# A third fold of the odd rows of a Fourier transform in seven of eight sequences: four row tiles, products of 94 or 95 columns

## The chip, the cores and the metric

The kernel runs on one core of one Trainium2 chip. The metric is the device time of one execution in microseconds (us); shown are medians of several runs. The engines are TensorE (PE; its weight loads are listed apart as PEld), VectorE (DVE), ScalarE (ACT), GpSimd (POOL) and SyncE (SP, which issues most DMAs). Each takes its own instructions in the order in which the program gave them, and they meet at semaphores.

## The reference

```python
x: (8, 3008, 256) float32          # batch, sequence, width
X = np.fft.fft(x, axis=1)
X = np.fft.fft(X, axis=2)
attn = X.real                      # (8, 3008, 256)
h = attn.reshape(24064, 256) @ w_in      # w_in (256, 2048)
r = np.maximum(h, 0.0)
out = (r * r) @ w_out                    # w_out (2048, 256)
```

So: the real part of a two-dimensional Fourier transform of every sequence, and then a two-layer network with a squared Relu.

## The kernel before, in words

**Two jobs interleaved.** The kernel goes through 8 sequences (b), each of 6 blocks of 251 (or 250) frequencies k, each block in 8 iterations j: 384 iterations in all. An iteration is `front` (two halves h; each makes two matmuls into a PSUM tile `ph`, of which there are two buffers; DVE adds them up in three instructions, `he` and twice `g`), `combine` (ACT: Relu and Square over `g`; POOL: four sums `s`) and, two iterations later, `back` (seven matmuls that add up in `mA` to `mD`). At the end of a block, `gather` and `store` bring the result out. The width transform is folded into the first weight matrix (`G1`, `G2`), so that the sequence transform alone is left to be made for each sequence: `Pt` (cosine part) and `Qt` (sine part).

**The transform of sequence b+1 is made while sequence b runs.** `ahead(b)` writes out a list of pieces, each with a weight that stands for its time. `between()`, called after each half h of a front, takes pieces from the list at an even pace, so that the list is used up at the sequence's end. For one iteration in each block (two iterations after the block's start) no pieces are taken. The first sequence has fewer calls for its list (53 against 78), because its first 8 iterations also convert the weights, and takes pieces at a quarter of the pace until iteration 16. Its list is longer too: it has the column of the middle frequency (`fold_columns`, `dft_ops(None)`) and the tables' reordering (`part_table`).

**The sequence transform by folds.** Only rows n from 0 to S/4 are needed, since x[n], x[S-n], x[S/2-n] and x[S/2+n] come as four rows of one tile and are added and subtracted first (`fold`: `f_s`, `f_d`, `f_sc`, `f_dc`, `f_w`; about 4 us of DVE for a tile). The rows stand in classes: n divisible by four, n = 2 mod 4, other small odd ones, and a last class (c = 3, `ODD0` and after) which holds the rows from S/8 + 1 to S/4, 376 of them. For each of cosine and sine (`which`) and for even and odd k (`kp`) a `group` makes an `even_n` product, joins it (`join_4`, `join_2`), makes the `odd_n` product, and joins both (`join_1`). That is four groups for each sequence. The products go into PSUM tiles `pd` (two buffers).

**The second fold.** In sequences 1 to 7 the class c = 3 is folded once more, row r with row 2*HALF - r, by `f_turn`, `f_even`, `f_sine` and `f_odd` in `fold`: the rows that come mirrored are loaded in blocks of 32 in reverse order, and `stream_shuffle` reverses each block. The even columns are added and subtracted, the odd ones turned through an angle that the table `turn` holds for every row. The products then have half of the columns (189 or 188), in two parts. `once_more` makes them: for c = 3, two parts by two row tiles of 128 rows, four matmuls in each group. Class c = 2 is treated so too, with rows tiles `TWO` and `TWO + 1` of 94 rows, and products of 94 or 95 columns. For kp = 1, each such product needs a copy to SBUF by ACT and two DVE instructions (`join_odd`) to put it together; for kp = 0 the two parts are written into every other column of PSUM directly.

**What sets the order.** The program order on each engine is the order in which the pieces are emitted. A piece that waits holds up whatever its engine was given after it. The x tiles are loaded by SP three tiles ahead (`NX`), each load emitted with `f_d` of an earlier tile. `make_turn` fills `turn` by ACT at iteration 8 (i == NJ), before that iteration's front.

Of the kernel before, what the change touches and what calls it, by code (L numbers as in the profile page):

```python
# [8 lines left out]
F32 = mybir.dt.float32  # L9
# [5 lines left out]
R = 32  # L15
# [67 lines left out]
def kernel(  # L83
# [54 lines left out]
    ODD0 = NT - 3  # L138
    HALF = S // 16
    REST = HALF - P  # L140
    ODD = [[(0, 0, P)],
           [(p, 2 * HALF - p - R, R) for p in range(0, P, R)],
           [(0, P, H // 2)] + [(H // 2 + p, 2 * HALF - P - p - R, R) for p in range(0, H // 2, R)]]
    assert H == P and REST <= H // 2 and TILES[ODD0][0] == 3 and TILES[ODD0 + 1][1] == TILES[ODD0][1] + P

    TWO = ODD0 - 2
    HALF2 = S // 32
    ROWS2 = TILES[TWO][3]
    assert TILES[TWO][0] == TILES[TWO + 1][0] == 2 and HALF2 <= ROWS2 < HALF2 + R and ROWS2 % R == 0

    def load_x(b, t):
        c, r0, step, rows = TILES[t]
        if b and c == 3:
            xt[b, t] = xp.tile([P, 4, D], F32, name="xt", tag="x")
            for p, first, count in ODD[t - ODD0]:
                nc.sync.dma_start(out=xt[b, t][p:p + count], in_=x[b, S // 8 + 1 + first:S // 8 + 1 + first + count])
            return
        if b and t == TWO + 1:
            xt[b, t] = xp.tile([P, 4, D], F32, name="xt", tag="x")
            for p in range(0, ROWS2, R):  # L160
                at = TILES[TWO][1] + step * (2 * HALF2 - p - R)
                nc.sync.dma_start(out=xt[b, t][p:p + R], in_=x[b, at:at + step * (R - 1) + 1:step])
            return

        while rows % 15 and rows % 16 and r0 + step * rows < NROW:
            rows += 1

        pool, tag = (gp, "g") if b == 0 and t < NT - NX else (xp, "x")
        xt[b, t] = pool.tile([P, 4, D], F32, name="xt", tag=tag)
        nc.sync.dma_start(out=xt[b, t][0:rows], in_=x[b, r0:r0 + step * (rows - 1) + 1:step])  # L170

    cosd = const.tile([P, 2, P], F32, name="cosd")
# [152 lines left out]

    turn = const.tile([P, 3, 3], F32, name="turn")

    def make_turn():
        for i, t in enumerate((ODD0, ODD0 + 1, TWO)):
            for a, tab in enumerate((cosT, sinT, sinT)):  # L330
                r = slice(0, TILES[t][3])
                nc.scalar.mul(turn[r, a, i:i + 1], tab[r, 1, PLACE[t]:PLACE[t] + 1], -1.0 if a == 2 else 1.0)

    rows_used = const.tile([P, 1], F32, name="rows_used")
    nc.vector.memset(rows_used, 0.0)
    nc.vector.memset(rows_used[0:REST], 1.0)

    def part_table(tab, t):


        nk, at = NC[0][TILES[t][0]], PLACE[t]
        rows = TILES[t][3]
        v = tab[0:rows, 0, at:at + nk]
        a = op.tile([P, nk], F32, name="tp", tag="os")[0:rows]
        nc.scalar.mul(a, v, rows_used if t == ODD0 + 1 else 1.0)
        nc.scalar.copy(v[:, 0:(nk + 1) // 2], a[:, 0::2])
        nc.scalar.copy(v[:, (nk + 1) // 2:], a[:, 1::2])

    def columns(tab, t, part):

        nk, at = NC[0][TILES[t][0]], PLACE[t]
        nq = (nk + 1) // 2
        return tab[:, 0, at + part * nq:at + (nk if part else nq)]

    NE = B - 1
# [20 lines left out]
    def fold(b, t):  # L376


        odd, two = b > 0 and t >= ODD0, b > 0 and t == TWO + 1
        r = slice(0, P if odd else ROWS2 if two else TILES[t][3])  # L380
        st = {}
# [12 lines left out]
        def f_d():  # L394
            v = xt[b, t]
            tt(out=new(fp, "fd", [P, 2, D])[r], in0=v[r, 0::3], in1=v[r, 1:3], op=ALU.subtract)
            if b > 0 and b * NT + t + NX < B * NT:
                load_x(*divmod(b * NT + t + NX, NT))

# [29 lines left out]
        ops = [(0.9, f_s), (0.9, f_d), (0.7, f_sc), (0.6, f_dc), (1.1, f_w)]  # L429
        if not (odd or two) or t == ODD0:  # L430
            return ops, None


        i = 2 if two else t - ODD0 - 1
        rows = slice(0, (P, REST, HALF2)[i])

        def f_turn():
            w = w_of(t)
            if i != 1:
                st["v"], st["w"] = w_of(t - 1), w  # L440
                nc.vector.stream_shuffle(w[r], w[r], REVERSE)
            else:
                st["v"], st["w"] = w, w_of(NT)
                nc.vector.stream_shuffle(st["w"][0:H // 2], w[H // 2:P], REVERSE)
                nc.gpsimd.memset(st["w"][H // 2:P], 0.0)
            spare("f0", "f0")
            nc.scalar.copy(st["f0"][rows], st["v"][rows, 0])

        def spare(nm, tag):
            st[nm] = fp.tile([P, D], F32, name=nm, tag=tag, bufs=1)  # L450
            return st[nm]

        def sine(to, src, signs):
            for part, a in zip(PART, signs):
                nc.scalar.mul(to[rows, part], src[rows, 1, part], turn[rows, 1 + a, i:i + 1])

        def f_even():
            v, w, a = st["v"][rows, 0], st["w"][rows, 0], st["f0"][rows]
            tt(out=v, in0=a, in1=w, op=ALU.add)
            tt(out=w, in0=a, in1=w, op=ALU.subtract)  # L460

        def f_sine():
            sine(spare("f1", "f1"), st["w"], (0, 1))
            sine(spare("f2", "f0"), st["v"], (1, 0))

        def f_odd():
            for nm, u in (("f1", "v"), ("f2", "w")):
                u = st[u][rows, 1]
                nc.vector.scalar_tensor_tensor(out=u, in0=u, scalar=turn[rows, 0, i:i + 1], in1=st[nm][rows],
                                               op0=ALU.mult, op1=ALU.add)  # L470

        return ops + [(0.8, f_turn), (1.3 if odd else 0.7, f_even), (0.2, f_sine)], (1.4 if odd else 1.2, f_odd)

    def dft_ops(b):
# [7 lines left out]
        def group(kp, which):  # L482
# [25 lines left out]
            def even_n():  # L508
                st["ps"] = psd.tile([P, 512], F32, name="pd", tag="d")[0:n]
                for c, at, nk in EVEN:  # L510
                    if b and c == 2:
                        st["half"] = once_more(st["ps"][:, at:], c, nk)
                    else:
                        product(st["ps"][:, at:at + nk], c)
                copy_4()
# [49 lines left out]

            def once_more(ps, c, nk):

                nq = (nk + 2) // 2 if kp else (nk + 1) // 2
                pairs, rows = ((((TWO, TWO + 1),), HALF2), (((ODD0, ODD0 + 1), (ODD0 + 2, NT)), P))[c == 3]
                for part in range(2):  # L570
# [3 lines left out]
                    else:  # L574
                        tab, o = (cosT, sinT)[which], part
                        to = ps[:, part:nk:2]
                    for i, pair in enumerate(pairs):
                        nc.tensor.matmul(to, folded[b, pair[part != which]][0:rows, kp, PART[which]][:, 0:n],  # L578
                                         columns(tab, pairs[0][i] if c == 3 else TWO, o)[0:rows],
                                         start=i == 0, stop=i == len(pairs) - 1)  # L580
                if not kp:
# [3 lines left out]
                return a, ps[:, nq:2 * nq]  # L585

            def odd_n():
                ps = psd.tile([P, 512], F32, name="pd", tag="d")[0:n]
                st["odd"] = ps[:, 0:n0]
                if b is None:  # L590
                    return product(ps[:, 0:n0], 3)
                st["odd"] = once_more(ps, 3, n0)

# [31 lines left out]
            if b and kp:  # L625
                ops.insert(4, (0.5, lambda: join_odd("odd", n0)))
                ops.insert(2, (0.4, lambda: join_odd("half", n1)))
            return ops

# [161 lines left out]
    def ahead(b):  # L791
        start, *groups = dft_ops(b)
        if b == 1:

            tables = [(0.3, lambda tab=tab, t=t: part_table(tab, t)) for t in (TWO, ODD0, ODD0 + 1)
                      for tab in (cosT, sinT)]
            groups = [(1.5, fold_columns)] + dft_ops(None) + tables + groups
        groups.insert(0, start)

        pieces = []  # L800
        for ops, last in [fold(b, t) for t in range(NT)] + [(groups + [(0.0, lambda: load_e(b))], None)]:
            if held:
                ops.insert(3, held.pop())
            if last:
                held.append(last)
            pieces += ops
        return pieces

    held = []

# [130 lines left out]
    for i in range(len(steps) + LAG + 4):  # L941
        if i < len(steps):
            b, k0, n, j = steps[i]
            if i == NJ:
                for t in range(NX):
                    load_x(1, t)
            if NJ <= i < NJ + NT:
# [92 lines left out]
```

## Time and profile before

| | |
|---|---|
| median of 3 runs | 1938.28 us (1938.12 to 1938.69) |
| span of the profiled execution | 1936.6 us |
| granted TensorE clock, mean | 1.000 |
| PE busy, 242 to 1694 us (windows of 48 to 242 us) | the whole of each window |
| fronts and backs of an iteration on PE | 22 records of 251 columns, 4.67 us |
| period of a sequence (710.24 to 943.21 us, the same product twice) | 232.97 us |
| DMA, mean share of the engines in the middle of the run | 0.11 |

The profile is one execution. An instruction's row tells its source line, engine, operation, the tiles it writes and reads, its shape, the count, the busy time, the mean length and the idle time of the engine before it. PE's rows overlap, since a matmul's end is modelled; its pace is read from the differences of starts. An fp32 matmul stands in the trace as two records. The weight loads (PEld) run beside the matmuls.

### The profile page before, as it was taken

To read this page: it belongs to the slowest core of one execution; us is meant where nothing else is said; L and a number is where in the kernel's file an instruction comes from. 1 tells how busy PE (TensorE), PEld (TensorE's weight loads), DVE (VectorE), ACT (ScalarE), POOL (GpSimd) and SP (SyncE) were. 2 spreads that over 40 slices of the span, in tenths; PEclk is the share of its full clock that TensorE was granted. 3 is DMA by queue.
4 is the path that set the end of the run, shared out by engine and by line. 5 is a ranking of instruction groups with operands and counts; after the bars stand their busy time and mean duration, and the time that the engine had idled before them with its cause. 6 is when DMAs were issued, how large, how long until landed. Compare 5 with 4: busy or idle time off the path is not lost.

```text
span 1936.6 us, 27913 instructions
## 1 busy us (share of the span) xinstructions
PE 1922.7 (99%) x9266; PEld 1708.9 (88%) x9266; DVE 1424.4 (74%) x3502; ACT 939.5 (49%) x1134; POOL 1185.6 (61%) x1708
## 2 busy tenths in 40 slices
PE   8999999999999999999999999999999999999999
PEld 7788888888988899888998889888898888988887
DVE  8998867777677776787667776777767787655554
ACT  2855554544445544445444454445544454444443
POOL 0047646676567665766667665667756776556655
PEclk9999999999999999999999999999999999999999
DMA  8341101111011101111011100111001100000000
GB/s 216 115 48 41 39 8 51 33 32 27 27 41 31 38 12 30 39 41 28 11 35 47 36 20 11 42 48 28 20 17 52 33 11 22 28 12 11 22 11 22
DMA packets 145783, 69.56 MB, mean 36 GB/s; under 512 B 129309, under 2 KB 136423, under 8 KB 145638
## 3 DMA queue, kind: packets, MB, share of 16 engines
q1 hardware_dynamic: 145186, 66.87, 13.3%
q8 instruction: 73, 1.20, 0.3%
q0 software_dynamic: 176, 0.65, 0.1%
q14 instruction: 72, 0.59, 0.1%
q10 hardware_dynamic: 276, 0.26, 0.0%
HBM read 43.03 MB, written 24.69 MB: 35 GB/s over the span
## 4 chain that ended last, share of the span: by engine, by line
PE 95%; DVE 3%; DMA 1%; issue 0%; SPq 0%; ACT 0%; DVEq 0%
PE ph L664 17%; PE ph L665 16%; PE mC L717 16%; PE mA L717 16%; PE mB L717 16%; PE mD L717 8%; PE pd L578 2%; PE pd L501 1%; DMA cosT<-in_cos_s_dram 0%; DVE m L274 0%; DVE he L667 0%; DMA cosd<-in_cos_d_dram 0%; DVE fd L272 0%; DVE g L670 0%; PE mA L704 0%
## 5 line engine op out<-in xcount | busy, mean ns | idle before, releaser
L679 ACT ACTIVATE g<-g 128x1004 f32<-128x1004 f32 (+1 forms) x384 | 399.4, 1040 | 783.6 <-DVE g L670 419.1
L667 DVE SCALAR_TENSOR_TENSOR he<-Et,gE,ph 128x251 f32<-128x251 f32 (+1 forms) x768 | 361.6, 471 | 385.4 <-PE ph L665 382.0
L687 POOL TENSOR_TENSOR s<-g 128x251 f32<-128x251 f32 (+1 forms) x376 | 249.0, 662 | 640.6 <-ACT g L680 507.2
L664 PE MATMUL ph<-Pt,G 128*128 128x251 f32 (+1 forms) x1536 | 451.9, 375 | 0.2 <-DVE g L670 0.2
L665 PE MATMUL ph<-Qt,G 127*128 127x251 f32 (+1 forms) x1536 | 451.3, 374 | 0.0
L680 ACT ACTIVATE g<-g 128x1004 f32<-128x1004 f32 (+1 forms) x384 | 399.3, 1040 | 12.1
L717 PE MATMUL mC<-s,wsum 128*128 128x251 f32 (+1 forms) x1504 | 381.4, 374 | 0.0
L717 PE MATMUL mA<-g,wout 128*128 128x251 f32 (+1 forms) x1504 | 379.9, 374 | 0.0
L669 DVE TENSOR_TENSOR g<-he,ph 128x251 f32<-128x251 f32 (+1 forms) x768 | 320.5, 417 | 54.5 <-DVE he L667 0.9
L665 PEld LDWEIGHTS ph<-Qt,G 127*128 127x128 f32 x1536 | 291.3, 190 | 35.7
L664 PEld LDWEIGHTS ph<-Pt,G 128*128 128x128 f32 x1536 | 286.7, 189 | 36.2 <-DVE dc L547 1.3
L717 PEld LDWEIGHTS mC<-s,wsum 128*128 128x128 f32 x1504 | 285.5, 190 | 34.5
L670 DVE TENSOR_TENSOR g<-he,ph 128x251 f32<-128x251 f32 (+1 forms) x768 | 314.1, 409 | 0.0
L717 PEld LDWEIGHTS mA<-g,wout 128*128 128x128 f32 x1504 | 282.6, 189 | 35.0 <-issue 0.3
L689 POOL TENSOR_TENSOR s<-g 128x251 f32<-128x251 f32 (+1 forms) x376 | 303.3, 807 | 0.0
L688 POOL TENSOR_TENSOR s<-s,g 128x251 f32<-128x251 f32 (+1 forms) x376 | 280.1, 745 | 29.5
L690 POOL TENSOR_TENSOR s<-g,s 128x251 f32<-128x251 f32 (+1 forms) x376 | 260.6, 693 | 0.0
L717 PE MATMUL mB<-g,wsum 128*128 128x251 f32 (+1 forms) x752 | 220.4, 374 | 0.0
L717 PE MATMUL mD<-s,wout 128*128 128x251 f32 (+1 forms) x752 | 220.3, 374 | 0.0
L717 PE MATMUL mB<-s,wout 128*128 128x251 f32 (+1 forms) x752 | 219.9, 374 | 0.0
L717 PEld LDWEIGHTS mB<-g,wsum 128*128 128x128 f32 x752 | 142.5, 190 | 17.5
L717 PEld LDWEIGHTS mD<-s,wout 128*128 128x128 f32 x752 | 141.9, 189 | 17.7
(139 smaller groups left out, 1353.9 us busy)
## 6 DMA issues: line engine op xcount, KB each, us to landing
out_dram<-os SPq DMA_DIRECT2D x376, 56.0 KB
xt<-in_x_dram SPq DMA_DIRECT2D x25, 384.0 KB
xt<-in_x_dram SPq DMA_DIRECT2D x63, 128.0 KB
Et<-e_dram SPq DMA_DIRECT2D x7, 752.5 KB
xt<-in_x_dram SPq DMA_DIRECT2D x9, 512.0 KB
out_dram<-os SPq DMA_DIRECT2D x288, 6.8 KB
raw<-in_moe_w_in_dram SPq DMA_DIRECT2D x16, 256.0 KB
raw<-in_moe_w_out_dram SPq DMA_DIRECT2D x16, 256.0 KB
```

The source lines that it names most:

```text
L664: nc.tensor.matmul(hP, G1[:, fs], pt[:, ks], start=True, stop=True)
L665: nc.tensor.matmul(hQ, G2[0:P - 1, fs], qt[0:P - 1, ks], start=True, stop=True)
L667: nc.vector.scalar_tensor_tensor(out=t, in0=et[:, ks], scalar=gE[:, fc:fc + 1], in1=hP, op0=ALU.mult, op1=ALU.add)
L669: tt(out=g[:, h, 0, 0:n], in0=t, in1=hQ, op=ALU.add)
L670: tt(out=g[:, h, 1, 0:n][:, ::-1], in0=t, in1=hQ, op=ALU.subtract)
L679: act(v, v, AF.Relu)
L680: act(v, v, AF.Square)
L687: gt(out=s1, in0=g21, in1=g22, op=ALU.add)
L688: gt(out=s2, in0=s1, in1=g11, op=ALU.subtract)
L689: gt(out=s3, in0=g11, in1=g21, op=ALU.subtract)
L690: gt(out=s4, in0=g12, in1=s2, op=ALU.subtract)
L717: nc.tensor.matmul(acc[nm][:, i, 0:n], w, v[:, 0:n], start=j == 0 and i == 0, stop=j == NJ - 1, skip_group_check=True)
```

## The change

In sequences 1 to 7 the class c = 3 is folded a third time, row n with S/8 - n. There are now four row tiles of 96 rows (94 used), named av, aw, bv and bw, instead of three of 128, 128 and 120; each passes through `fold`. Then `once` (what `f_turn` to `f_odd` did) joins av with aw and bv with bw, and, as before, the two tiles of class 2; and `twice` joins the two pairs: sums and differences of halves of the even-k columns (`even`), a turn of the differences by a second angle (`sine` on ACT, `turned` on DVE), and sums and differences of the odd-k columns (`copies` on ACT, `odd_v` and `odd_w`). `twice_more` makes the products: four matmuls in each group still, but each of 94 or 95 columns with 94 rows. For kp = 0 they are written to every fourth column of PSUM, and `join_turned` (one ACT copy, two DVE instructions) puts two of the four parts together.

The table `turn` gets a fourth angle, computed by three DVE instructions from two that ACT wrote, and scaled by ACT. The tiles are taken in another order (`ORDER`), and `ahead` weaves the steps of `once` and `twice` between the steps of later folds. The weights of the list for one sequence are the times written beside the pieces.

```diff
+    NL = ODD0 + 4
+    ODD = [[(0, 0, ROWS2)],
+           [(p, 4 * HALF2 - p - R, R) for p in range(0, ROWS2, R)],
+           [(p, 2 * HALF2 - p - R, R) for p in range(0, ROWS2, R)],
+           [(0, 2 * HALF2, ROWS2)]]
...
+    ORDER = [TWO, TWO + 1, 0, *range(ODD0, NL), 1]
...
     def make_turn():
-        for i, t in enumerate((ODD0, ODD0 + 1, TWO)):
+        for i, t, kp, k in ((BY_AC, ODD0, 1, 0), (BY_TWO, TWO, 1, 0), (BY_AB, ODD0, 0, 1)):
             for a, tab in enumerate((cosT, sinT, sinT)):
-                r = slice(0, TILES[t][3])
-                nc.scalar.mul(turn[r, a, i:i + 1], tab[r, 1, PLACE[t]:PLACE[t] + 1], -1.0 if a == 2 else 1.0)
+                r = slice(0, ROWS2)
+                nc.scalar.mul(turn[r, a, i:i + 1], tab[r, kp, PLACE[t] + k:PLACE[t] + k + 1], -1.0 if a == 2 else 1.0)
+        c, z = (turn[0:ROWS2, a, BY_AC:BY_AC + 1] for a in range(2))
+        for a, (u, v, op) in enumerate(((c, z, ALU.add), (c, z, ALU.subtract), (z, c, ALU.subtract))):
+            to = turn[0:ROWS2, a, BY_BD:BY_BD + 1]
+            tt(out=to, in0=u, in1=v, op=op)
+            nc.scalar.mul(to, to, 0.5 ** 0.5)
...
+    def twice(v, w, v2, w2):
...
+        def begin():
+            a = st["a"] = spare("f0")
+            nc.scalar.copy(a[:, p], v[:, 0, p])
+            nc.scalar.copy(a[:, q], w[:, 0, q])
+
+        def even():
+            butterfly(v[:, 0, p], v2[:, 0, p], st["a"][:, p])
+            butterfly(w[:, 0, q], w2[:, 0, q], st["a"][:, q])
+
+        def sine():
+            f, f2 = st["f"] = spare("f1"), spare("f0")
+            for to, u, part, a in ((f, w2, p, SIN), (f2, w, p, LESS), (f, v2, q, LESS), (f2, v, q, SIN)):
+                nc.scalar.mul(to[:, part], u[:, 0, part], by(BY_AB, a))
+
+        def turned():
+            f, f2 = st["f"]
+            for u, part, to in ((w, p, f), (w2, p, f2), (v, q, f), (v2, q, f2)):
+                mix(out=u[:, 0, part], in0=u[:, 0, part], scalar=by(BY_AB, COS), in1=to[:, part],
+                    op0=ALU.mult, op1=ALU.add)
+
+        def copies():
+            st["a"], st["b"] = spare("f0"), spare("f1")
+            nc.scalar.copy(st["a"], v[:, 1])
+            nc.scalar.copy(st["b"], w[:, 1])
+
+        def odd_v():
+            butterfly(v[:, 1], v2[:, 1], st["a"])
+
+        def odd_w():
+            butterfly(w[:, 1], w2[:, 1], st["b"])
...
+            def twice_more(ps):
...
+                av, aw, bv, bw = (folded[b, ODD0 + i] for i in range(4))
+                if kp:
+                    nq = (n0 + 2) // 2
+                    spots = [(tab, part, ps[:, i * nq + part:(i + 1) * nq:2])
+                             for i, tab in enumerate((cosT, sinT)) for part in range(2)]
+                    ws = (aw, bw, bv, av) if which else (av, bv, bw, aw)
+                else:
+                    tab = (cosT, sinT)[which]
+                    spots = [(tab, 0, ps[:, 0:n0:4]), (tab, 1, ps[:, 2:n0:4]),
+                             (cosT, 0, ps[:, 1:n0 + 1:4]), (sinT, 0, ps[:, 3:n0:4])]
+                    ws = (bw, aw, bv, av) if which else (av, bv, aw, bw)
+                for (tab, part, to), w in zip(spots, ws):
+                    cols = quarters(tab, part)
+                    nc.tensor.matmul(to, w[0:HALF2, kp, PART[which]][:, 0:n], cols[:, cols.shape[-1] - to.shape[-1]:],
+                                     start=True, stop=True)
...
+            def join_turned():
+                a, up, down = st["turned"]
+                tt(out=up, in0=a, in1=down, op=ALU.add)
+                if which == 1:
+                    tt(out=down, in0=down, in1=a, op=ALU.subtract)
+                else:
+                    tt(out=down, in0=a, in1=down, op=ALU.subtract)
...
+        two = later(lambda: once(w(TWO), w(TWO + 1), BY_TWO))((0.1, 0.9, 0.2, 1.0))
+        first = later(lambda: once(w(av), w(aw), BY_AC))((0.1, 0.9, 0.2, 1.0))
+        second = later(lambda: once(w(bv), w(bw), BY_BD) + twice(w(av), w(aw), w(bv), w(bw)))(
+            (0.1, 0.9, 0.2, 1.0, 0.1, 1.2, 0.2, 1.2, 0.2, 0.9, 0.9))
+        return (fold(b, TWO) + fold(b, TWO + 1) + woven(fold(b, 0), two) + fold(b, av) + fold(b, aw)
+                + woven(fold(b, bv), first) + fold(b, bw) + woven(fold(b, 1), second)
+                + [start] + groups + [(0.0, lambda: load_e(b))])
```

## The prediction

> **What bounds the kernel now.** I read the page first (busy shares, then the chain of waits), then the busy time by window, then the timeline of single engines. The busy shares and the chain:
>
> ```profile
> PE 1922.7 (99%) x9266; PEld 1708.9 (88%) x9266; DVE 1424.4 (74%) x3502; ACT 939.5 (49%) x1134; POOL 1185.6 (61%) x1708
> PE 95%; DVE 3%; DMA 1%; issue 0%; SPq 0%; ACT 0%; DVEq 0%
> ```
>
> TensorE (PE) carries the end: 95% of the chain. The windows (stretch in us, its length, then busy time of PE, weight load, DVE, ACT, POOL) say where anything else can matter:
>
> ```profile
> 97.00:145.00 48.00, 47.98 (x226) 42.27 (x225) 45.04 (x115) 25.06 (x36) 23.46 (x35) 1.00 0.40 48
> 145.00:194.00 49.00, 48.81 (x231) 43.09 (x230) 43.58 (x101) 24.96 (x30) 36.26 (x49) 1.00 0.16 41
> 194.00:242.00 48.00, 48.00 (x228) 39.94 (x227) 42.49 (x103) 24.46 (x34) 33.18 (x47) 1.00 0.15 39
> ...
> 484.00:726.00 242.00, 242.00 (x1167) 216.57 (x1166) 179.76 (x443) 115.78 (x137) 157.10 (x224) 1.00 0.11 30
> ```
>
> From 97 us on PE is never free, at full clock. So PE work taken away is time won, as long as DVE keeps up. In a steady sequence DVE is busy 74%; while the first transform is prepared (97 to 242 us) it is 89 to 94%.
>
> The price of the matmuls, from PE's timeline (start, length, line, shapes, count; an fp32 matmul leaves two records):
>
> ```profile
> 716.02 0.58 PE L501 MATMUL pd<-cosT,w 95*128 95x94 f32 x4
> 716.44 0.39 PE L578 MATMUL pd<-cosT,w 94*128 94x95 f32 x2
> 716.66 0.39 PE L578 MATMUL pd<-sinT,w 94*128 94x95 f32 x2
> 716.89 0.62 PE L664 MATMUL ph<-Pt,G 128*128 128x251 f32 x2
> 717.34 0.59 PE L665 MATMUL ph<-Qt,G 127*128 127x251 f32 x2
> ...
> 737.78 1.44 PE L578 MATMUL pd<-sinT,w 128*127 128x189 f32 x8
> 739.06 0.59 PE L664 MATMUL ph<-Pt,G 128*128 128x250 f32 x2
> ```
>
> Lengths overlap, so take differences of starts. An odd group of now (eight records of 188 or 189 columns) takes 739.06 - 737.78 = 1.28 us, 160 ns a record. Eight records of 94 or 95 columns take 716.89 - 716.02 = 0.87 us; the four with 94 rows alone 0.45, so 111 ns a record. Half the columns is not half the time.
>
> [...] the strided 128x189 products of kp=0 (710.08 to 711.35 us, eight records) run at 159 ns, like the contiguous ones of kp=1. A step of four is in no row.
>
> **PE's part.** The group keeps four matmuls (eight records), now 94 or 95 columns. After is between 0.87 and 0.90 us, plus 0.025 because the next pair of front matmuls waits for its weights (717.34 - 716.89 = 0.45, against 0.425 after a long product). Taken: 0.91, so 0.37 saved, times 4 groups times 7 sequences: **10.4 us**. Bounds: 10.9 with 0.89; if the step-of-four outputs (half the groups) are slow, down to 160 ns a record: 14 x 8 x 0.05 = 5.6 less, so 4.8. I take no slowing, from the step of two.
>
> **DVE's part, per sequence.** By-form rows give the durations, two of them here:
>
> ```profile
> L422 DVE TENSOR_TENSOR w<-sc 96x256 f32<-96x256 f32 x28 | 20.9, 784 | 0.1
> L469 DVE SCALAR_TENSOR_TENSOR w<-w,turn,f 94x256 f32<-94x256 f32 x14 | 9.3, 702 | 0.0
> ```
>
> One fold more, of 96 rows: L392 0.71, L396 0.78, L408 0.57, L412 0.47, L422 2 x 0.75 (20.9/28) = 4.0; three folds go from 128 to 96 rows: 0.2 each less, net 3.5. `twice` adds four half-width adds and four full ones (full 0.62, the mean of L459 and L460 at 94x256, half estimated 0.33): 1.3 + 2.5; four half-width L469s (full 0.66, half estimated 0.38): 1.5. `join_turned`: 4 x 0.25 (L547 at 128x94). Shuffles and the three `once` stay as they were. Sum **9.8 us**. POOL loses a memset of 0.5; ACT gains some 3.5 (eight copies and scalings of 0.24 to 0.39) at 49% busy; DMAs of x stay at 8 for the odd rows, only in another order and three tiles ahead. These three I cost at nothing: their cover is ACT's and the queues' idle time.
>
> In a steady sequence, DVE goes from 74% to (172.6 + 9.8)/231.5 = 79%. What PE tolerates follows from this timeline:
>
> ```profile
> 709.23 0.58 PE L664 MATMUL ph<-Pt,G 128*128 128x251 f32 x2
> 710.27 0.48 DVE L667 SCALAR_TENSOR_TENSOR he<-Et,gE,ph 128x251 f32<-128x251 f32 x1 [1.05 <-PE ph L665]
> 711.19 0.41 DVE L670 TENSOR_TENSOR g<-he,ph 128x251 f32<-128x251 f32 x1
> ```
>
> DVE frees a `ph` buffer 711.60 - 709.23 = 2.4 us after its front starts, and the second 1.3 later. PE comes back to them one iteration (4.67 us) later: at 4.67 and 5.52. That leaves 2.3 and 1.8 us in an iteration for side pieces between the halves. The paced pieces rise from 49.1/78 = 0.63 to 57.2/78 = 0.73 units a call, and a piece is at most 1.4 us. I find no iteration of a steady sequence that overruns: cost 0. Where a piece waits for ACT (`even`, `turned`, `odd_v`), ACT's Relu and Square (2.1 us) are mostly over when DVE has done its next three front operations; at most some tenths.
>
> **The first sequence: two losses.** First, `make_turn`. It now has three DVE subtractions and additions of [96,1] that need the second ACT scaling. They stand on DVE ahead of the first front of that iteration. DVE first, ACT second:
>
> ```profile
> 99.43 0.42 DVE L267 TENSOR_SCALAR m<-raw 128x512 uint32<-128x512 uint32 x1
> 99.77 0.47 DVE L667 SCALAR_TENSOR_TENSOR he<-Et,gE,ph 128x251 f32<-128x251 f32 x1
> ...
> 105.23 0.47 DVE L667 SCALAR_TENSOR_TENSOR he<-Et,gE,ph 128x251 f32<-128x251 f32 x1
> ```
>
> ```profile
> 102.57 1.04 ACT L680 ACTIVATE g<-g 128x1004 f32<-128x1004 f32 x1
> 103.51 0.19 ACT L332 ACTIVATE turn<-cosT 128x1 f32<-128x1 f32 x1
> 103.61 0.28 ACT L332 ACTIVATE turn<-sinT 128x1 f32<-128x1 f32 x2
> ```
>
> ACT reaches the scalings at 103.5, behind three conversion steps and the Relu and Square of the iteration before; the second ends near 103.8. DVE, free at 99.8, waits until then and needs some 0.35 for the three: `he` moves from 99.77 to about 104.25, **4.5 us** of DVE. Queued behind: the front's additions, the last weight conversion, the sums of w_out. The `he` of 105.23 moves to 109.7, its first buffer is free at 111.0, and PE wanted it at 108.70: 2.3 late, about 3.0 after the next iteration's second buffer. Both sides: 0 if DVE could be late without PE noticing (its 1.8 us of spare are less than 4.5, so no), 4.5 if no spare helps.
>
> Second, from 97 to 242 us DVE idles 145 - 131.1 = 13.9 us. Some 0.07 us behind each `he` (L669's idle before, 54.5/768) can't be filled: 62 x 0.07 = 4.3. So 9.6 are left for 4.5 of waiting plus 8.8 (9.8 without `join_turned`): 3.7 too few, and PE ends that stage at least that late. Paced calls there rise from 56.2/53 = 1.06 to 63.7/53 = 1.20 units; pieces come in lumps, so I add 1.5. Loss **5.2** (3.0 at the turn, 2.2 after); bounds 2 and 9.
>
> **Sum.** 1936.6 - 10.4 + 5.2 = 1931.4 for the span; the median lies 1.7 above the profiled span, so 1938.3 - 5.2 = **1933.0**.
>
> **Rivals.**
> - The start costs little (DVE's idle takes more of it, loss 0 to 2.5): 1928 to 1930.5. For it: DVE idles in some iterations of the stage. Against it: the next iteration with idle time (141 us, DVE 61% busy) is nine iterations after the wait.
> - The loss eats the gain: strided outputs slow (5.6) or the start costs 9: 1935 to 1942. For it: no row shows a step of four. Against it: the step of two costs nothing.
> - Slower: DVE waits for ACT in `twice` in every sequence. `even`, `sine`, `turned` stand there with no other piece between. If DVE reaches `turned` while ACT has Relu and Square (2.1) and four scalings (1.6) ahead, it waits 3.6, 1.8 over PE's spare; times 7 is 12.6: 1945.6. It decides from 0.75 us of PE a sequence. Against it: the pieces are mostly popped in different calls.
>
> **Chances.** The forecast (loss 2.5 to 7) 0.50, the start costs little 0.14, the loss eats the gain 0.24, slower 0.12. A measurement tells 0.2% (3.9 us) from no change. Faster is the first two but for 0.04 near the edge: 0.60; within 0.2%: 0.28; slower: 0.12. The range, 1929 to 1941, leaves out the slow case and the far ends of the two rivals before it, some 0.07.
>
> **What shows it.** Right: odd groups of 0.9 us in PE's timeline; a DVE wait on ACT of about 4 us before the `he` near 100 us with PE late by 3 behind it; PE without a gap past 300 us, with a period of 231.5 instead of 233.0 us a sequence. Wrong: records of 94 columns at over 120 ns where the step is four, PE gaps on `ph` in steady sequences, or no wait at the turn.

## The result and the profile after

| | before | after |
|---|---|---|
| median, same chip, 12 runs each | 1938.42 us (1936.53 to 1939.55) | 1939.43 us (1937.57 to 1940.77) |
| ratio after/before | | 1.0006 (95%: 0.9997 to 1.0014) |
| span of the profiled execution | 1936.6 us | 1937.4 us |
| first sequence: first front to first front of the second | 259.28 us | 268.50 us |
| the six sequences after it | 1397.74 us | 1388.62 us |
| start up to the first front, and the end | | 0.2 and 0.4 us longer |

No change that can be measured. The forecast was 1933.0 and faster; the time lies inside the range of 1929 to 1941. The last three rows say what happened: the gain is there, 9.1 us in six sequences, and the first sequence gives all of it back. (The start, up to the first front, moves by some 3 us between executions, in the traces of the later runs from 41.7 to 44.9 us. So single traces are compared here by stretches that begin after it.)

The page of after, busy shares and the chain of waits (shares of the span by engine):

```profile
PE 1916.4 (99%) x9266; PEld 1699.7 (88%) x9266; DVE 1498.2 (77%) x3657; ACT 957.4 (49%) x1201; POOL 1178.7 (61%) x1701
PE 93%; DVE 4%; DMA 1%; SPq 1%; issue 1%; ACT 0%; POOL 0%; DVEq 0%; POOLq 0%
```

PE has 6.3 us less to do, and two points of the chain have gone from PE to other engines. DVE has 73.8 us more. The windows of after say where (stretch, length, busy time of PE, weight load, DVE, ACT, POOL; then granted clock, DMA share, GB/s):

```profile
97.00:145.00 48.00, 46.18 (x207) 39.28 (x206) 42.03 (x109) 23.03 (x36) 20.68 (x30) 0.96 0.38 37
145.00:194.00 49.00, 48.50 (x229) 42.79 (x228) 45.92 (x105) 25.63 (x31) 36.28 (x50) 1.00 0.20 44
194.00:242.00 48.00, 46.96 (x221) 41.48 (x220) 44.99 (x105) 25.99 (x39) 32.30 (x46) 1.00 0.18 40
242.00:290.00 48.00, 44.77 (x225) 35.43 (x224) 32.42 (x91) 21.81 (x41) 21.46 (x34) 0.96 0.05 8
484.00:726.00 242.00, 242.00 (x1183) 216.50 (x1182) 191.03 (x467) 120.05 (x149) 157.83 (x226) 1.00 0.15 31
```

In the steady window PE is busy throughout, with DVE at 79%. All that PE lacks is missing between 97 and 290 us, in two places above all, and in exactly the two windows that hold them the clock stands at 0.96.

**The first place: `make_turn`.** DVE's timeline of after, then PE's (start, length, line, shapes, count; in brackets the idle time before it and what ended it):

```profile
99.71 0.42 DVE L277 TENSOR_SCALAR m<-raw 128x512 uint32<-128x512 uint32 x1
104.08 0.30 DVE L349 TENSOR_TENSOR turn<-turn 96x1 f32<-96x1 f32 x3 [3.96 <-ACT turn L345]
104.30 0.47 DVE L766 SCALAR_TENSOR_TENSOR he<-Et,gE,ph 128x251 f32<-128x251 f32 x1
...
110.52 0.46 DVE L766 SCALAR_TENSOR_TENSOR he<-Et,gE,ph 128x251 f32<-128x251 f32 x1
```

```profile
105.60 0.69 PE L763 MATMUL ph<-Pt,G 128*128 128x251 f32 x2 [1.57 <-DVE g L769]
106.13 0.59 PE L764 MATMUL ph<-Qt,G 127*128 127x251 f32 x2
106.76 1.02 PE L763 MATMUL ph<-Pt,G 128*128 128x251 f32 x2
107.58 1.04 PE L764 MATMUL ph<-Qt,G 127*128 127x251 f32 x2
108.78 1.18 PE L803 MATMUL mA<-g,wout 128*128 128x251 f32 x2 [0.16 <-DVE wout L285]
```

DVE waits 3.96 us for ACT's scaling, and `he` comes at 104.30, where before it came at 99.77. PE waits 1.57 us for the `ph` buffer. Then comes what was not foreseen: a matmul of two records that took 0.59 us at 106.13 takes 1.04. The records of the granted clock show half speed from 106.98 to 110.40 us.

**The second place: the hand-over from folds to products.** PE's timeline of after, and DVE's for the same stretch:

```profile
237.43 0.69 PE L763 MATMUL ph<-Pt,G 128*128 128x251 f32 x2 [1.04 <-DVE g L769]
...
242.64 0.69 PE L763 MATMUL ph<-Pt,G 128*128 128x251 f32 x2 [0.27 <-DVE g L769]
243.17 0.59 PE L764 MATMUL ph<-Qt,G 127*128 127x251 f32 x2
246.43 1.63 PE L564 MATMUL pd<-cosT,we 95*7 95x95 f32 x8 [2.67 <-DVE we L397]
247.99 2.04 PE L816 MATMUL mA<-g,wout 128*128 128x251 f32 x4
```

```profile
244.02 0.43 DVE L766 SCALAR_TENSOR_TENSOR he<-Et,gE,ph 128x251 f32<-128x251 f32 x1
...
245.21 0.43 DVE L395 TENSOR_TENSOR es<-xe 128x98 f32<-128x98 f32 x1
245.67 1.38 DVE L397 TENSOR_TENSOR we<-es 128x49 f32<-128x49 f32 x2
```

DVE is behind with the last folds, so that `fold_columns` (L395, L397) comes late, and PE's product of the columns follows right on it in the program. It waits 2.67 us. Again the clock is halved, from 246.93 to 250.34 us: the four records of `mA` take 2.04 us. The same two instructions in PE's timeline of before, without a wait:

```profile
231.63 1.14 PE L501 MATMUL pd<-cosT,we 95*7 95x95 f32 x8
...
233.66 1.01 PE L717 MATMUL mA<-g,wout 128*128 128x251 f32 x4
```

Cut into stretches, by the starts of the first `Pt` matmul of each iteration (us; the last three columns are experiments told below):

| iterations | before | after | both moves | both, less DVE | both, other weights |
|---|---|---|---|---|---|
| 8 to 10 | 10.50 | 14.61 | 10.49 | 10.50 | 10.49 |
| 10 to 20 | 46.77 | 46.78 | 46.78 | 46.78 | 47.85 |
| 20 to 22 | 9.35 | 10.12 | 10.12 | 10.11 | 9.78 |
| 22 to 36 | 65.88 | 65.43 | 65.43 | 65.43 | 67.08 |
| 36 to 39 | 20.93 | 26.86 | 23.55 | 21.58 | 21.89 |
| 39 to 48 | 50.81 | 49.65 | 49.65 | 49.65 | 51.84 |
| 48 to 96, a steady sequence | 232.98 | 231.43 | 231.43 | 231.43 | 232.58 |

The turn costs 4.1 us, iterations 20 to 22 0.8, iterations 36 to 39 5.9. The first sequence became 9.2 us longer; it has saved 1.5 as every other, so its loss is 10.7, against a saving of 7 x 1.52 = 10.6 in all.

### The profile page after: what moved, and what is told of

Read it like the earlier page. It is cut to its first block, busy times and chain, and to the rows that moved or that the text cites. A ratio compares the mean times of both kernels' runs of the same rounds, so it can differ in the third digit from the quotient of the medians.

```text
span 1937.4 us, 28151 instructions
## 1 busy us (share of the span) xinstructions
PE 1916.4 (99%) x9266; PEld 1699.7 (88%) x9266; DVE 1498.2 (77%) x3657; ACT 957.4 (49%) x1201; POOL 1178.7 (61%) x1701
## 4 chain that ended last, share of the span: by engine, by line
PE 93%; DVE 4%; DMA 1%; SPq 1%; issue 1%; ACT 0%; POOL 0%; DVEq 0%; POOLq 0%
PE mA L816 16%; PE mC L816 16%; PE mB L816 16%; PE ph L763 16%; PE ph L764 16%; PE mD L816 8%; PE pd L564 2%; PE pd L666 1%; PE pd L640 1%; DVE he L766 1%; DVE g L769 0%; DMA cosT<-in_cos_s_dram 0%; DVE m L284 0%; DVE g L768 0%; DVE fd L282 0%
## 5 line engine op out<-in xcount | busy, mean ns | idle before, releaser
L786 POOL TENSOR_TENSOR s<-g 128x251 f32<-128x251 f32 (+1 forms) x376 | 244.8, 651 | 652.7 <-ACT g L779 574.1
L768 DVE TENSOR_TENSOR g<-he,ph 128x251 f32<-128x251 f32 (+1 forms) x768 | 320.5, 417 | 52.9 <-ACT g L778 0.5
L787 POOL TENSOR_TENSOR s<-s,g 128x251 f32<-128x251 f32 (+1 forms) x376 | 292.0, 776 | 29.5
L788 POOL TENSOR_TENSOR s<-g 128x251 f32<-128x251 f32 (+1 forms) x376 | 294.4, 783 | 0.0
```

What stands on the lines that cost most here:

```text
L768: tt(out=g[:, h, 0, 0:n], in0=t, in1=hQ, op=ALU.add)
L786: gt(out=s1, in0=g21, in1=g22, op=ALU.add)
L787: gt(out=s2, in0=s1, in1=g11, op=ALU.subtract)
L788: gt(out=s3, in0=g11, in1=g21, op=ALU.subtract)
```

## The experiments

The theory after the result, called A: two places in the first sequence take what seven sequences win, `make_turn` and the hand-over, where DVE is late; the steady sequences lose nothing. The rivals, B in most runs: a delay that is taken away comes back later in the same sequence, because DVE has too much to do there in any case, or the change has costs in the steady sequences too. Medians of the kernel before beside the runs lay between 1938.66 and 1938.82, where it was 1938.42 beside the kernel after; so what is said "by medians" against the kernel after is good to some tenths of a microsecond.

**The fourth angle later.** The three DVE instructions and their scalings move from iteration 8 to iteration 16, when ACT has long written what they read.

```diff
         def make_turn():
...
+    def make_turn_bd():
         c, z = (turn[0:ROWS2, a, BY_AC:BY_AC + 1] for a in range(2))
...
+            if i == 2 * NJ:
+                make_turn_bd()
```

> The fourth angle is computed eight iterations later (iteration 16), when ACT has long scaled the others. Theory A (separate losses at the start: the wait for ACT costs PE 4.1 us, of which some 1.7 is the stretch at half clock that PE's idle time brings on): 1939.4 - 4.1 = 1935.3, and no half-clock stretch near 107 us. Theory B (DVE is short of time in the whole stage, so that PE, freed of the early wait, waits later for the same DVE work): 1938 to 1939.4, the start of the second sequence's fronts no earlier than 311 us. A part of both would be 1936 to 1937.5.

Measured: 1935.07 us (1933.89 to 1936.2), ratio to before 0.998 (0.9972 to 0.9988). Iterations 8 to 10 take 10.51 us, and no later stretch is longer than in after: 4.1 us came out in the trace, 4.4 by medians. A holds for the turn.

**The columns earlier.** In the first list, `fold_columns` stands ahead of the last but one fold instead of straight ahead of its product.

```diff
-            groups = [(1.5, fold_columns)] + dft_ops(None) + tables + groups
+            groups = dft_ops(None) + tables + groups
...
+        columns_1 = [(1.5, fold_columns)] if b == 1 else []
...
-                + woven(fold(b, bv), first) + fold(b, bw) + woven(fold(b, 1), second)
+                + woven(fold(b, bv), first) + columns_1 + fold(b, bw) + woven(fold(b, 1), second)
```

> fold_columns is taken before the fold of bw, so that PE's first product of the middle column no longer follows right behind the DVE additions that it needs. Theory A: the 2.7 us of PE idle before that product and its half-clock stretch (1.7) go: 1939.4 - 4.4 = 1935.0. Theory B (DVE short of time): DVE is as late as before, PE waits at the next front or product instead: 1938 to 1939.4.

Measured: 1935.65 us (1933.96 to 1937.57), ratio 0.9984 (0.9977 to 0.9991). Iterations 36 to 39 go from 26.86 to 23.55; the wait for `we` is gone, and in this trace so is the half clock there. (It can come back: the run with more DVE work, below, has the same order in these iterations, a half-clock stretch at 241.95 us, and 25.19 us for them. So the move itself is worth 1.7 us, and 3.3 where the clock stays up.) But 2.6 us over before stay: A for the larger part, B for the rest.

This trace shows one thing more. Its turn is that of the kernel after, and PE waits there as long, but no half clock follows:

```profile
105.70 0.69 PE L763 MATMUL ph<-Pt,G 128*128 128x251 f32 x2 [1.56 <-DVE g L769]
...
107.39 0.59 PE L764 MATMUL ph<-Qt,G 127*128 127x251 f32 x2
108.88 0.66 PE L803 MATMUL mA<-g,wout 128*128 128x251 f32 x2 [0.91 <-DVE wout L285]
```

PE runs on at full speed into a wait of 0.91 us for the converted weights, where in the kernel after it came slower and waited 0.16. Iterations 8 to 10 take 13.79 us instead of 14.61, iterations 10 to 22 take 57.58 instead of 56.90: from 8 to 22 the half clock is worth 0.1 us.

**Both moves together.**

> Both edits. Theory A: 1939.4 - 8.5 = 1930.9, clock 1.000 throughout. Theory B: over 1936. If the lost time were not in the first sequence at all (rival C: it is spread over the steady sequences), 1939.

Measured: 1933.13 us (1931.18 to 1935.6), ratio 0.9971 (0.9962 to 0.9981). This beats both kernels: 5.7 us below the one before, and by medians 6.3 below the one after. 2.2 us of what A expected are missing. PE's waits between 97 and 302 us in this run (who waits for whom, us in total, times, the longest):

```profile
PE ph L765 <- DVE g L771: 2.9, 3, 1.7
PE pd L566 <- DVE dc L610: 0.3, 1, 0.3
```

**The wait alone, in the kernel before.** To the old `make_turn` come three additions of [96,1] on DVE that read ACT's scalings, and three scalings by ACT; nothing reads what they give.

```diff
+        for a in range(3):
+            tt(out=turn_x[0:96, a:a + 1], in0=turn[0:96, 0, 0:1], in1=turn[0:96, 1, 0:1], op=ALU.add)
+            nc.scalar.mul(turn_x[0:96, a:a + 1], turn_x[0:96, a:a + 1], 0.5 ** 0.5)
```

> The kernel before with three DVE additions and three ACT scalings added to make_turn, whose results nothing uses: the wait alone, without the third fold. Theory A: 1938.4 + 4.1 = 1942.5, with a half-clock stretch near 107 us. Theory B: the stage of the kernel before has DVE time to spare, so PE catches up nothing but waits only at the turn: 1940.5 to 1942.5 as well; if PE's spare of 1.8 us and DVE's idle take most of it, 1939 to 1940.

Measured: 1943.17 us (1941.79 to 1944.36), ratio 1.0022 (1.0013 to 1.0032). DVE's timeline of this kernel:

```profile
103.73 0.29 DVE L335 TENSOR_TENSOR turn_x<-turn 96x1 f32<-96x1 f32 x3 [3.95 <-ACT turn L333]
103.95 0.46 DVE L671 SCALAR_TENSOR_TENSOR he<-Et,gE,ph 128x251 f32<-128x251 f32 x1
```

The same wait, and iterations 8 to 10 take 14.64 us. Without a single matmul or fold changed, three DVE instructions of 0.29 us together cost 4.4 us by medians. From both sides, taken away and put in, the turn is worth the same.

**More calls for the list.** Both moves, and the first sequence's list is spread over 56 calls instead of 53, so that DVE gets less in each.

```diff
-                calls = 2 * (NJ - 1) * (len(BLOCKS) - (0 if i else 2)) - 6 + (0 if i else (NJ - LAG) // 2)
+                calls = 2 * (NJ - 1) * (len(BLOCKS) - (0 if i else 2)) - 6 + (0 if i else (NJ - LAG) // 2 + 3)
```

> The version with both edits (1933.1), and in the first sequence the pieces are taken at a pace that is 5% lower (56 calls in place of 53), so that they end later, in iterations that had none. Theory A (what is left of the loss, 2.6 us around 240 us and 0.8 at 160 us, is DVE running late by lumps of pieces): 1931 to 1932.5. Rival: the lost time is there whatever the pace, or comes back when the last pieces end just ahead of the next sequence's first front: 1933 to 1935.

Measured: 1934.14 us (1932.12 to 1934.63), ratio 0.9973 (0.9963 to 0.9984): no gain, the expectation missed. PE's waits on `ph` between 97 and 302 us are now six, 4.2 us together, where both moves alone had three: iterations 36 to 39 fell to 18.50 us, with the product of the columns now behind them, and 20 to 48 as a whole took 151.0 against 148.75.

**Part of the work on POOL.** Both moves; the sums over w_out of every second iteration from 8 to 15 are made by POOL, and iterations 8 to 15 take pieces at half pace instead of a quarter.

```diff
+        minus = tt if j % 2 else nc.gpsimd.tensor_tensor
-        tt(out=t3, in0=b22, in1=b12, op=ALU.subtract)
+        minus(out=t3, in0=b22, in1=b12, op=ALU.subtract)
...
-        spent -= pace / 4 if i < 2 * NJ else pace
+        spent -= pace / 2 if i < 2 * NJ else pace
...
-                calls = 2 * (NJ - 1) * (len(BLOCKS) - (0 if i else 2)) - 6 + (0 if i else (NJ - LAG) // 2)
+                calls = 2 * (NJ - 1) * (len(BLOCKS) - (0 if i else 2)) - 6 + (0 if i else NJ - LAG)
```

> The version with both edits, and the sums of w_out of every second iteration from 8 to 15 on POOL in place of DVE, and twice the pace of pieces in those iterations. If DVE's time in that stage is what is short, 8 us less of it give 1930 to 1931.5. Rival: POOL's work slows DVE's and the Strassen sums of the iteration itself (POOL's pieces stand in the way of back): 1933 to 1937.

Measured: 1933.02 us (1931.65 to 1933.52), ratio 0.9969 (0.9957 to 0.998): no change. Iterations 36 to 39 won 1.3 us, iterations 10 to 20 lost 1.4. The delay only moved, as B expects, but the sums and the pace were changed at once, so this run alone tells little.

**Work for PE while it waits.** The kernel after, with idle 128-column matmuls, 6 ahead of the front that waits at the turn and 10 ahead of the product of the columns. PE still waits for the same DVE instructions, but it isn't idle.

```diff
+            if i == NJ + 1:
+                busy(6)
...
-            groups = [(1.5, fold_columns)] + dft_ops(None) + tables + groups
+            groups = [(1.5, fold_columns), (0.0, lambda: busy(10))] + dft_ops(None) + tables + groups
```

> The changed kernel (1939.4) with idle matmuls for PE in its two long waits: 6 of 128 columns ahead of the front of iteration 9, 10 between fold_columns and the first product of the middle column. Nothing else moves. If the half-clock stretches after these waits are a cost of their own (0.8 us at the first, 1.7 at the second, from the lengths of the same iterations with and without), 1936.9 and no stretch near 107 and 247 us in the profile. Rival: the waits alone cost, the clock is only their trace: 1939 to 1941.

Measured: 1937.44 us (1935.72 to 1939.72), ratio to before 0.9995 (0.9987 to 1.0003), by medians 2.0 less than after. PE's timeline of this kernel at the hand-over:

```profile
242.43 2.39 PE L893 MATMUL pd<-ident 128*128 128x128 f32 x20
245.26 1.14 PE L564 MATMUL pd<-cosT,we 95*7 95x95 f32 x8 [0.44 <-DVE we L397]
246.33 1.11 PE L816 MATMUL mA<-g,wout 128*128 128x251 f32 x4
```

`mA` takes 1.11 us, not 2.04. Iterations 8 to 10 fell from 14.61 to 13.77, 36 to 39 from 26.86 to 25.23, and the records show no half speed in either place. At the hand-over the half clock costs 1.6 us beside the waits ahead of it, and nothing later takes that back. At the turn the 0.8 us are won only for a moment: iterations 10 to 22 lost 0.7 of them again (57.57 us for 56.90), the same as in the run with the earlier columns. PE waits for DVE there either way.

**More DVE work in the steady sequences.** Both moves, and 16 additions of 128x256 in each of the sequences two to seven, which nothing reads: 9.3 us of DVE by their row (0.579 each).

```diff
+        extra = (0.65, lambda: tt(out=cosd, in0=sind, in1=sind, op=ALU.add))
```

> The version with both edits (1933.1), and 16 more DVE additions of 128x256, 0.65 us each and used by nothing, among the folds of each of the six steady sequences: 10.4 us of DVE a sequence, as much as the third fold added. Theory: DVE has room there (79% to 84% busy), no change, 1932.5 to 1934. Rival: the steady sequences are close to the edge too, so that each loses 0.5 to 2 us: 1936 to 1945.

Measured: 1934.18 us (1932.7 to 1936.51), ratio 0.9976 (0.9967 to 0.9984). The period rises from 231.43 to between 231.79 and 231.89 us. Another 9 us of DVE, nearly as much as the change itself added to a sequence, cost 0.4 us there. In the first sequence the change's own 10 us, with the wait at the turn, cost far more. This fits the theory that room for DVE work is what the two differ in.

**Less DVE work in the first sequence.** Both moves, and `turned`, `odd_v` and `odd_w` are left out in the first of the seven transforms.

```diff
+        if b == 1:
+            turned = odd_v = odd_w = lambda: None
         return begin, even, sine, turned, copies, odd_v, odd_w
```

> Both moves (as in the run with the later angle and the earlier column), and in the first of the seven transforms alone the steps turned, odd_v and odd_w of twice are left out, so one sequence comes out wrong: about 4 us of DVE work less (four mixes of half a width, four additions of a full one), all of it between 145 and 240 us. Theory A (what is left of the loss after both moves is DVE's work itself, more than the first sequence has room for): the 3.4 us that iterations 20-22 and 36-39 still take over the kernel before go, and the time is near 1930.0; the period of the later sequences stays at 231.43. Theory B (they are due to where pieces stand in front of PE's products, not to how much DVE has to do): at most 1 us is won, 1932.0 to 1933.5.

Measured: 1930.01 us (1929.9 to 1931.3), ratio 0.9953 (0.9941 to 0.9966). PE's waits on `ph` between 97 and 302 us:

```profile
PE ph L767 <- DVE g L773: 1.2, 2, 0.7
```

By medians 3.1 us less than both moves, in the two traces 1.9, nearly all of it in iterations 36 to 39 (21.58 for 23.55). Iterations 20 to 22 stay at 10.11: what was left out comes after them. The time that A gave came to the hundredth, but 1.2 us of it are not in these two traces, so that is luck in part. Nor does this run alone tell A from B: `turned` stands right in the stretch that got shorter, so a large piece went from a bad place together with the work. What speaks for the amount is the other runs: a slower pace, work on POOL, and the larger weights below all shorten iterations 36 to 39 too, but leave the first sequence as long as with both moves or longer (263.35, 261.40 and 263.96 us against 261.05, first front to first front); only less work made it shorter (259.13).

**Weights nearer to the truth.** Both moves, and the steps of `once` and `twice` carry larger weights in the list.

```diff
-        two = later(lambda: once(w(TWO), w(TWO + 1), BY_TWO))((0.1, 0.9, 0.2, 1.0))
-        first = later(lambda: once(w(av), w(aw), BY_AC))((0.1, 0.9, 0.2, 1.0))
+        two = later(lambda: once(w(TWO), w(TWO + 1), BY_TWO))((0.1, 1.3, 0.2, 1.5))
+        first = later(lambda: once(w(av), w(aw), BY_AC))((0.1, 1.3, 0.2, 1.5))
...
-            (0.1, 0.9, 0.2, 1.0, 0.1, 1.2, 0.2, 1.2, 0.2, 0.9, 0.9))
+            (0.1, 1.3, 0.2, 1.5, 0.1, 2.0, 0.2, 2.2, 0.2, 1.3, 1.3))
```

> Both moves, and the steps of once and twice stand in the list with weights nearer to what they take on DVE beside POOL (even 1.3 to 2.0, odd and turned 1.5 to 2.2, odd_v and odd_w 1.3, where it was 0.9 to 1.2), so that the list is paced more evenly in every sequence. Theory A (DVE has too little idle time in the first sequence, however it is spread): no change, 1932.5 to 1933.7. Theory B (the rest of the loss is lumps, pieces that cost more than their weight and come in the wrong iteration): 1 to 3 us less, 1930 to 1932. In the later sequences both expect 231.4 a sequence.

Measured: 1941.98 us (1940.64 to 1944.4), ratio 1.0016 (1.001 to 1.0023). Neither theory had this: the pieces' places moved in every sequence, and now each steady sequence has one wait of PE. In the steady window of its trace, ACT, DVE and PE at that place:

```profile
690.02 1.04 ACT L781 ACTIVATE g<-g 128x1004 f32<-128x1004 f32 x1
690.96 0.28 ACT L508 COPY f<-w 94x128 f32<-94x128 f32 x1
```

```profile
690.69 0.41 DVE L771 TENSOR_TENSOR g<-he,ph 128x251 f32<-128x251 f32 x1
691.28 0.64 DVE L471 TENSOR_TENSOR w<-f,w 94x128 f32<-94x128 f32 x1 [0.18 <-ACT f L508]
691.95 0.76 DVE L472 TENSOR_TENSOR w<-f,w 94x128 f32<-94x128 f32 x1
692.63 0.80 DVE L471 TENSOR_TENSOR w<-f,w 94x127 f32<-94x127 f32 x1
693.46 0.60 DVE L472 TENSOR_TENSOR w<-f,w 94x127 f32<-94x127 f32 x1
693.99 0.46 DVE L768 SCALAR_TENSOR_TENSOR he<-Et,gE,ph 128x251 f32<-128x251 f32 x1
```

```profile
695.28 0.69 PE L765 MATMUL ph<-Pt,G 128*128 128x251 f32 x2 [0.87 <-DVE g L771]
```

`even` (L471, L472) stands behind ACT's copy, which stands behind Relu and Square. It waits only 0.18 us, but its four additions take 2.8 us, and `he` comes 2.9 us after the `g` ahead of it has ended (691.10). That is more than the 1.8 to 2.3 us that PE can spare. The period is 232.58 us, 1.15 more than with the old weights; the first sequence is 2.9 longer. Here the truer weights made it worse; what decided is where a long piece falls.

## Why the prediction came out as it did

The time lies inside the range, but that is luck: the sum said 1933.0, 6.4 us too low, and faster, where no change came. The range holds because it took in a rival, the loss that eats the gain. Of the two halves of the sum, the saving was right and the loss of the first sequence (5.2 us, measured 10.7) was not.

**PE's saving (10.4 us): right.** In PE's timeline of after a group whose outputs step by four runs from 718.88 to 719.74 us, 0.86 us, and one whose outputs step by two from 730.01 to 730.88, 0.87; taken was 0.91, with 0.025 for the matmul after it. The chain of waits of after has the groups at 0.86 us, two of them a sequence apart:

```profile
719.04 0.86 PE pd L666 x8
...
950.46 0.86 PE pd L666 x8
```

Six sequences gained 1.52 us each, where 1.49 was taken. That a step of four costs nothing, taken from a step of two, held: 0.86 us beside 0.87. Nor does the trace of before show shorter weight loads for fewer rows: those of L578 with 128 columns take 192 ns each at 94 rows and 189 to 190 at 128.

**DVE's part (9.8 us a sequence) and no cost in steady sequences: right.** DVE has 73.8/7 = 10.5 us more, its share in the steady window is the 79% that was worked out, and between 302 and 1700 us the trace has no wait of PE. The run with 9.3 us more shows how far that goes. (Three sums of the prediction are off by 0.1, which changes nothing: the fold's net is 4.0 - 0.6 = 3.4, Relu and Square with four scalings are 3.7, and 1938.3 - 5.2 is 1933.1.)

**The turn (DVE 4.5 us, PE 3.0): the wait right, its price too low.** `he` at 104.30 was forecast at 104.25; the fronts of after start 0.2 us later, so DVE was late by 4.3 us. PE lost 4.1 us. The clock, a term that the sum did not have, is not the reason: in the two runs whose traces have no half clock at the turn, PE lost 3.3 us in iterations 8 to 10, near the forecast, but 0.7 more up to iteration 22. So nearly all that DVE was late came through to PE, close to the forecast's own limit "if no spare helps"; the spare that it counted on put off a part of the loss and saved some 0.3 us at most.

**After the turn (2.2 us): this step failed.** It measured 10.7 - 4.1 = 6.6 us. The step compared DVE's idle time over the whole of 97 to 242 us (9.6 us to be filled) with what DVE had to add (13.3), and took 1.5 for lumps. That let DVE catch up anywhere. It did not. In the windows of after DVE still idles 145 - 132.9 = 12.1 us; 3.96 of them are the wait for ACT and 4.3, by the prediction's estimate, the small gaps behind each `he`. That leaves 3.8 us unused, of which the trace has 2.6 as waits for PE and 0.5 as a wait for ACT: where they fell, the next instruction in DVE's order was not a fold. And DVE's lag was paid for mostly at one place, the hand-over, where the forecast looked at `ph` buffers alone. The product of the columns has no spare at all: DVE's `we` and PE's product are neighbours in the program. Taking that neighbourhood apart gave 3.3 us (1.6 of them the clock, by the run with idle matmuls and by the two traces of the moved columns with and without it; the rest the wait). What stayed of iterations 36 to 39, 2.6 us, fell by 2.0 when 4 us of DVE work were left out; whether their amount or their place counts there is argued, not shown. The 0.8 us in iterations 20 to 22 went only with the slower pace (9.35 us) and in part with the other weights (9.78), and in both came up elsewhere. In the trace of after a lump stands there: between a `g` that ends at 162.30 us and the next `he` at 164.73 DVE has three pieces of 0.87, 0.93 and 0.83 us, more than PE's spare, and PE waits 0.50 us for `ph`. That is read from the trace and was not tested.

Why lumps are larger than taken: the rows' means hide two lengths. The four mixes of `turned` in the timelines of after and of both moves, and POOL's in the latter:

```profile
237.29 1.13 DVE L521 SCALAR_TENSOR_TENSOR w<-w,turn,f 94x128 f32<-94x128 f32 x4
```

```profile
237.31 2.49 DVE L523 SCALAR_TENSOR_TENSOR w<-w,turn,f 94x128 f32<-94x128 f32 x4
```

```profile
237.32 0.71 POOL L789 TENSOR_TENSOR s<-s,g 128x251 f32<-128x251 f32 x1
237.99 0.76 POOL L790 TENSOR_TENSOR s<-g 128x251 f32<-128x251 f32 x1
238.72 0.67 POOL L791 TENSOR_TENSOR s<-g,s 128x251 f32<-128x251 f32 x1
```

In after POOL stands still from 236.07 to 239.66 us, and the four take 1.13 us; with POOL at work they take 2.49. So moving a piece can change what it costs.

**The rivals.** That the loss eats the gain is what came, though by the start alone, and beyond its bound of 9; the strided outputs had no part in it. That DVE waits for ACT in `twice` in every sequence did not come in after. The run with other weights shows it was near: there `even` fell in the wrong place, and 1.15 us a sequence were lost, less by waiting for ACT than by four additions beside POOL.

The sum with measured terms, all but the first read from the two traces: 1938.4 - 10.6 (seven sequences) + 4.1 + 6.6 + 0.6 (start and end) = 1939.1, beside the measured 1939.43.

## What to carry to other kernels

A saving that is won a little in each repetition can be given back in one passage: price the fullest passage of the critical engine's supplier by itself, piece by piece, and not by its idle time in sum. There, look first for an instruction of the bound engine that follows its supplier's without a buffer between, and move the supplier's work ahead of it; and look for an instruction of the supplier that waits for a third engine: here three of 0.3 us together, in the wrong place, cost 4. In this case some waits of the bound engine cost its clock too: half-speed stretches came after waits of 1.56 to 2.67 us, but not after all (none after one of 1.56 and one of 1.69), and cost 1.6 us where the engine had work to do and 0.1 where it went on waiting for its supplier.

## What the runs showed of the hardware

**The clock falls after some waits and not after others.** In the kernel after, half speed for 3.41 us followed PE's waits of 1.57 us at the turn and of 1.04, 0.27 and 2.67 us at the hand-over. With idle matmuls in the longest wait of each, neither place had it, and the mean clock of that trace is 1.000. But a wait as long did not always bring it; it depends on the run. The turn of the kernel after had no half clock in the trace with the earlier columns, after a wait of 1.56 us. Both moves showed none at the hand-over, after a wait of 1.69 us, and the run with more DVE work in later sequences, with the same waits there, had one at 241.95 us and 25.19 us instead of 23.55 for iterations 36 to 39.

**VectorE beside GpSimd.** In after the addition at L470 (94x256, both inputs in SBUF) took 0.82 us at 240.60 us, beside POOL, and 0.42 at 242.95, when POOL had just stopped; `g` (L768), with one input in PSUM, took 0.42 in the same stretch both times (239.49 and 241.84 us). Over the whole trace of after, L470 at this shape takes 0.42 us in the 8 cases with POOL idle and 0.73 to 0.83 in the 27 beside it, nearly twice as long. But not every such addition is hit: L469, of the same shape and from the same tiles, took 0.42 us at 240.15 with POOL at work, and from 0.41 to 0.93 in the 28 cases that POOL overlapped for most of their length. So the mean of a row mixes two lengths, and the longer one can make a piece too long for the time between two halves.
